# Attention bounds in wider passes, a new table of tiles, and earlier fillers in a fused attention and MLP kernel

## The chip, the cores and the metric

The kernel runs on one core of a Trainium2 chip. The core has five engines that run side by side and meet through semaphores: TensorE (PE, matmuls, whose weight loads the profile shows as PEld), VectorE (DVE), ScalarE (ACT), GpSimd (POOL) and SyncE (SP, which here only issues DMAs). The metric is the time of the whole program on the device in microseconds. The kernel before took 806.86 us, the median of 14 runs, which lie between 805.44 and 808.62.

## The reference

One layer norm feeds an attention block and an MLP; both results are added to the input. Attention has 32 heads of size 16 that share one set of keys and values. There are 2048 rows of width 512, and the MLP is 1792 wide.

```python
def _A_ref(x, wq, wk, wv, wo):
    q = (x @ wq).reshape(B, S, H, Dh).transpose(0, 2, 1, 3)
    k = x @ wk
    v = x @ wv
    scores = jnp.einsum("bhqd,bkd->bhqk", q, k) * (Dh ** -0.5)
    p = _softmax(scores, axis=-1)
    o = jnp.einsum("bhqk,bkd->bhqd", p, v)
    return o.transpose(0, 2, 1, 3).reshape(B, S, H * Dh) @ wo

def _B_ref(x, w1, b1, w2, b2):
    h = _gelu(jnp.einsum("bsd,df->bsf", x, w1) + b1)
    return jnp.einsum("bsf,fd->bsd", h, w2) + b2

xn = _layernorm(x, axis=-1)
return x + _A_ref(xn, ...) + _B_ref(xn, ...)
```

## The kernel before

**Tiles and units.** The rows of queries are cut into four token blocks of 512 (`NTB`, `TBW`), the heads into eight groups of four (`NGR`, `HG`), the keys into 16 tiles of 128 (`NT`). A score tile is one head, 128 keys and 512 queries: 128 x 512 numbers, which fill one bank of PSUM. There are 4 x 8 x 64 = 2048 of them, in the order token block, head group, key tile, head. Three successive tiles make a unit, so there are 683 units, some 171 for each token block and 21 for each head group. The scores of a unit are three matmuls (line 848), which go side by side into banks 0 to 2 or 3 to 5, by turns: the scores of unit u+2 can start once both engines have read the banks of unit u.

**Two ways to an exponential.** Most tiles go to ScalarE: one instruction (line 867) takes all such tiles of a unit, three or two, to the buffer `E`. In some units one tile, the first or the last, goes to VectorE instead[...]. It turns the scores into an integer whose bits, read as bf16, are a crude power of two (line 884, into `Dt`), and for batches of up to three tiles (`KB`) makes four shifted copies of it (line 899). Multiplied with five scaled copies of the values and summed, the five curves approximate the exponential. TensorE therefore has one matmul with values for a tile on ScalarE and five for a tile on VectorE, all at line 888, added up in bank 6. Which unit gives which tile to VectorE is written out in `DTAB`, a string with one character for each unit: a dot for none, 0 or 2 for the tile's place.

**Bounds.** Instead of a maximum over keys, softmax subtracts a bound that Cauchy and Schwarz give: it grows with the length of the query times the greatest length of a key. The queries of a head group are projected (`q_group`: 16 matmuls of line 563 into bank 7), copied to `QT` (line 742) and squared (line 744); the squares lie in slots 6 and 7 of the buffer `hb`, chosen by `sq`. `q_m` then sums the squares of a pair of groups with one small matmul each (line 557, into bank 7), takes a square root by integer arithmetic (line 970, into `mT`) and writes the result with four DMAs into a spare row of `QT`, so that the score matmul subtracts it by itself.

**Side work.** Everything else hangs beside the units. The list `side` says behind which unit's exp a piece may start: projections and bounds (`q_pair`), the two MLP layers (`h_mm`, then `h_chain` with the tanh of line 997, then `y_mm`), the output projection and stores (`out_tile`, `y_tile`). All these matmuls go to bank 7 too, which is one buffer, so each piece must be read out by VectorE before the next can start.

**What sets the order.** The kernel records all operations with what they read and write. `Prog.schedule` then gives every engine a fixed order, from costs and due times that are written in the code; `Prog.emit` puts a semaphore wait where an operand comes from another engine. Where its model of TensorE has a gap longer than `FILL_GAP`, and its own clock is past `FILL_FROM` microseconds, it puts in matmuls that add zeros (the filler, line 1169 in the profile), whose purpose is to keep the engine busy. Before the first values are projected, a second kind of filler runs (line 1167).

**The end of a group.** After 64 tiles `o_evac` copies bank 6 out (line 912), and the sums of the weights make a way through DRAM to become the rows of `rbc` (two halves by turns), by which line 923 divides. The very last group goes through `o_norm_last` instead: the reciprocals are spread over a buffer `rX` (line 949 on VectorE, line 951 on ScalarE) and transposed by TensorE.

Of the kernel before, what the change touches and what calls it, by code (L numbers as in the profile page):

```python
# [6 lines left out]
ACT = mybir.ActivationFunctionType  # L7
# [3 lines left out]
P = 128  # L11
# [17 lines left out]
D_FIRST = 3  # L29
FILL_GAP = 0.25  # L30
FILL_U = 0.8
FILL_FROM = 60.0
PV_MIN = 2
PV_S = 1
P1_ALLOW = -20.0
# [12 lines left out]
LCO = 0.0  # L48
PRO_FROM = 2.0
TBL = 1  # L50
DTAB = "....2..020..02..22...22.202220..20.00.0...220...222200..02200...2.02.2200.00220.02...20222.20...022.0000...2002.0.2.20000.000...2020.2220.0..20020....02.222.0022020..2...202.202202.02.222.....02.222.2022.000.22...20220.00.0222.2022...2220.02..2.2.0022......022...20.202002.2......02.0.000222.00.0..22.0..222..200000......2200.02202.000.22....2220.02.220.22220...22.2020.202202.022....2022.20022.0000.0....20222.220020....220..22..0...0.0..20.00.....022.20..20222.002....20220.20...22022.....0.20202.0.222.220....2220222.00222.2.22...222.0022.00222.0.20...2.020000.222.222.......202.0200.0...02......0...022...22.200....002.202...02.02.20...2022.22..20.020222...22202200..220.2000...."
Y_ALLOW = 8.0
H_ALLOW = 5.0
YT_ALLOW = (3,3,3,3)
# [371 lines left out]
def bass_parallel_sum__grouped_kv_mqa__dense_activation_gelu__prompt_kernel(  # L426
# [22 lines left out]
    TBW = 512  # L449
    NTB = S // TBW  # L450
    HG = 4
    NGR = H // HG
    NE, ND, KB = NE_ND_KB
    NOT, NPR = 3, 5
    NV = 1 + len(SPL_K)
    KZ = SPL_K.index(0)
    GAM = 128.0 / LN2 * 0.25
    bf, f32 = dt.bfloat16, dt.float32
    i16, i32 = dt.int16, dt.int32

    with ExitStack() as es:
        def sb(shape, dtype, name):
            return es.enter_context(nc.sbuf_tensor(name, shape, dtype))
# [23 lines left out]
        ident_f = sb([P, P], f32, "ident_f")  # L487
        selL = sb([P, 4], f32, "selL")
        rT = sb([P, 4, 4], f32, "rT")
        rX = sb([P, 4, P], f32, "rX")  # L490
        isc = sb([P, 1], f32, "isc")
        ibi = sb([P, 1], f32, "ibi")
        sel8 = sb([P, 8, 32], bf, "sel8")
# [20 lines left out]
        Vf = sb([P, NT, Dh], f32, "Vf")  # L514
        V1 = sb([P, NV, NT, 32], bf, "V1")
        QT = sb([P, NGR, TBW], bf, "QT")
        hb = sb([P, 8, TBW], bf, "hb")
        sqq = hb
        mT = sb([32, TBW], bf, "mT")
        E = sb([P, NE, TBW], bf, "E")  # L520
# [1 line left out]
        Of = sb([P, 2, TBW], f32, "Of")  # L522
        den = sb([P, 2, 16], f32, "den")
        rbc = sb([P, 2, TBW], f32, "rbc")
        rd_dram = nc.dram_tensor("rden_rows", [NTB * NGR, HG * TBW], f32).ap()
        oT = sb([P, NOT, TBW], bf, "oT")
        oTp = sb([P, NPR, TBW], bf, "oTp")
# [17 lines left out]
        def dve(fn, r=(), w=(), n=TBW, mode=1, allow=1.0, **kw):  # L545
            return add("dve", fn, r, w, occ=vcost(n, mode), lat=0.16, allow=allow, **kw)

        def act(fn, r=(), w=(), n=TBW, allow=0.0, **kw):
            return add("act", fn, r, w, occ=0.051 + n / 1.2e3, lat=0.22, allow=allow, **kw)
# [23 lines left out]
        for i in range(8):  # L573
            dma("sp", x_sb[:, 2 * i:2 * i + 2, :], x_view[:, 2 * i:2 * i + 2, :], f"d_x{i}",
                w=[("x", 2 * i), ("x", 2 * i + 1)], lat=2.3 + 0.5 * i, due=0.0)
# [8 lines left out]
        def setup(fn, r=(), w=(), occ=0.25, due=0.0, **kw):  # L584
# [18 lines left out]
              r=["wk_s", "wkp"], w=["wkp"], occ=0.45, due=2.0)  # L603
# [6 lines left out]
              r=["mrow"], w=["isc"], due=10.0)  # L610
        setup(lambda e: e.memset(crow[0:1, :], 1.13 * GAM * GAM), w=["crow"], due=10.0)
        setup(lambda e: e.memset(V1[:, :, :, Dh:32], 0.0), w=["V1"], occ=1.4, due=11.0)
        for v, c in enumerate((1.0,) + SPL_C):
# [3 lines left out]
              r=["mask4", "sel8"], w=["sel8"], due=12.0)  # L617
# [118 lines left out]
                          r=["wqp" if hq else "wqp0"] + tr(4 * tb, 4 * tb + 4), w=[B(bk)], **kw)  # L736

        def sq(hq):
            return 6 + hq % 2

        def q_evac(tb, hq, bk, **kw):
            dve(lambda e: e.tensor_copy(QT[:, hq, :], bank(bk)),  # L742
# [30 lines left out]
        for _, _, kind, a in sorted(steps, key=lambda s: s[:2]):  # L773
# [14 lines left out]
            r=[("std", LN_B[-1][0])] + ([("KT", ti) for ti in range(NT)] if TBL else []), w=["dum"], n=1600, due=1.0)  # L788
        dve(lambda e: e.tensor_reduce(kmx[:], kmax[:], AX.X, ALU.max), r=[("kmax", 0), ("kmax", NVA)], w=["kmx"], n=40, due=0.0)
        add("pe", lambda e: e.transpose(bank(3)[0:1, 0:P], kmx[:], ident_f[:]), r=["kmx", "ident_f"], w=[B(3)], occ=0.12, lat=0.22,  # L790
            due=0.0)
# [3 lines left out]
            r=["mrow"], w=[B(3), "ibi"], n=40, due=0.0)  # L795
        q_first_m(0, 7)
        dve(lambda e: e.tensor_copy(R2[:], bank(3)[:, 256:257]), w=[B(3), "R2"], n=40)
        for va, vb_ in ((0, NVA), (NVA, NT)):
# [3 lines left out]
                due=22.0)  # L802
            dve(lambda e, va=va, vb_=vb_: e.tensor_copy(V1[:, 0, va:vb_, 0:Dh], Vf[:, va:vb_, :]), r=["V1", ("Vf", va)], w=[("V", 0, va)],
                n=(vb_ - va) * Dh, due=22.1)
        for v, c in enumerate(SPL_C):
            setup(lambda e, v=v, c=c: e.tensor_scalar(V1[:, 1 + v, :, 0:Dh], Vf[:], c, None, ALU.mult),  # L806
                  r=["V1", ("Vf", 0), ("Vf", NVA)], w=[("V", 1 + v, 0), ("V", 1 + v, NVA)], occ=0.45, due=20.0)

        setup(lambda e: e.tensor_copy(wqp[:, :, 4:H, 0:Dh], wq_s[:, :, 64:D].rearrange("p k (h n) -> p k h n", n=Dh)),  # L809
              r=[("u", i) for i in range(8, 12)] + ["wqp"], w=["wqp"], occ=2.7, due=19.0, after=[pr.writer["ibi"]])  # L810
        setup(lambda e: e.tensor_scalar(sel8R[:], sel8[:], R2[:, 0:1], None, ALU.mult),
              r=["sel8", "R2"], w=["sel8R"], occ=0.5, due=22.0)
# [118 lines left out]
                    r=[("oT", gg % NOT)], w=[("oTp", pp % NPR, h, j)])  # L931

        def o_norm_last(gg):
            tb, g = divmod(gg, NGR)
            for h in range(2):
                c = slice(h * 256, h * 256 + 256)
                dve(lambda e, c=c: e.tensor_copy(Of[:, 0, c], pO[:, c]), w=["O", ("Of", 2 * h)], n=256, due=0.0)
            for h in range(2):
                for i in (2 * h, 2 * h + 1):
                    mm(bank(h)[:, 4 * i:4 * i + 4], Of[:, 0, i * P:(i + 1) * P], selL[:], True, True,  # L940
                       r=[("Of", 2 * h), "selL"], w=[B(h)], occ=0.2, due=0.0)
            for h in range(2):
                dve(lambda e, h=h: e.reciprocal(rT[:, 2 * h:2 * h + 2, :],
                                                bank(h)[:, 8 * h:8 * h + 8].rearrange("p (i j) -> p i j", j=4)),
                    w=[B(h), ("rT", h)], n=100, due=0.0)
                o = rX[:, 2 * h:2 * h + 2, :].rearrange("p i (j r) -> p i j r", j=4)
                i_ = rT[:, 2 * h:2 * h + 2, :].unsqueeze(3).to_broadcast([P, 2, 4, 32])
                if h == 0:
                    dve(lambda e, o=o, i_=i_: e.tensor_copy(o, i_), r=[("rT", h)], w=[("rX", h)], n=256, due=0.0)
                else:  # L950
                    act(lambda e, o=o, i_=i_: e.activation(o, i_, ACT.Copy), r=[("rT", h)], w=[("rX", h)], n=256, due=0.0)
            for h in range(2):
                for i in (2 * h, 2 * h + 1):
                    add("pe", lambda e, i=i, h=h: e.transpose(bank(h)[:, 128 + (i % 2) * P:256 + (i % 2) * P], rX[:, i, :], ident_f[:]),
                        r=[("rX", h), "ident_f"], w=[B(h)], occ=0.15, lat=0.22, due=0.0)
            for h in range(2):
                c = slice(h * 256, h * 256 + 256)
                dve(lambda e, h=h, c=c: e.tensor_tensor(oT[:, gg % NOT, c], Of[:, 0, c], bank(h)[:, 128:384], ALU.mult),
                    r=[("Of", 2 * h)], w=[B(h), ("oT", gg % NOT) if h == 0 else ("oTl", 1)], n=256, due=0.0)
# [6 lines left out]
        def q_m(tb, hqs, **rel):  # L966
            pq = tb % 2
            for n, hq in enumerate(hqs):
                mm(pM[0:32, :], sel8R[:, hq, :], sqq[:, sq(hq), :], n == 0, n == len(hqs) - 1, r=["sel8R", ("h", sq(hq))], w=[M4[0]], tp=(0, 0), kind="side", tag=(None, 0))
            dve(lambda e: e.tensor_scalar(mT[:].bitcast(i16), pM[0:32, :].bitcast(i32),  # L970
                                          0.5 / 65536.0, float(0x1fc00000) / 65536.0, ALU.mult, ALU.add),
                w=M4 + ["mT"], allow=EV_ALLOW)
            h0, n = hqs[0], len(hqs)
            for j in range(4):
                dst = QT[32 * j + 16:32 * j + 17, h0:h0 + n, :]
                dma("sp", dst, mT[8 * j + h0:8 * j + h0 + n, :], f"d_m{j}",
                    r=["mT"] + [("QT", hq) for hq in hqs], w=[("QTm", hq, j) for hq in hqs])
# [72 lines left out]
        def at(u, fn, cost=0.0):  # L1050
            side.append((u, len(side), fn, cost))

        def q_pair(tb, hqs, u):
            for i, hq in enumerate(hqs):
                at(u + 1.5 * i, lambda tb=tb, hq=hq: q_group(tb, [hq], {}), 0.93)
            at(u + 1.5 * len(hqs), lambda tb=tb, hqs=hqs: q_m(tb, list(hqs)), 0.6)

        q_pair(0, (1,), 0)
        q_pair(0, (2, 3), 3)
# [3 lines left out]
        for tb in range(NTB):  # L1063
            u0 = tb * UPT
            if tb > 0:
                for i in range(4):
                    at(u0 + 3 + (YS if tb < NTB - 1 else 9) * i, lambda tb=tb, i=i: out_tile(tb - 1, i), 0.6)
                q_pair(tb, (6, 7), u0 + 50)
            a, b = (HA, HB) if tb < NTB - 1 else (LA, LB)
            if tb == 0:  # L1070
                a = 18
            nf = FT if tb < NTB - 1 else FT - FIN_F
            for f0 in range(0, nf, 3):
                fts = list(range(f0, min(nf, f0 + 3)))
                for ft in fts:
                    at(u0 + a + (b - a) * ft / FT, lambda tb=tb, ft=ft: h_mm(tb, ft), 0.6)
                at(u0 + a + (b - a) * fts[-1] / FT, lambda tb=tb, fts=fts: h_chain(tb, fts), len(fts) * 1.067 + 0.33)
            if tb + 1 < NTB:
                for k in range(3):
                    q_pair(tb + 1, (2 * k, 2 * k + 1), u0 + 46 + 42.7 * k)  # L1080
            else:
                for i in range(4):
                    at(u0 + LS + LY * i, lambda tb=tb, i=i: y_tile(tb, i), 0.6)
                fts = list(range(nf, FT))
                for ft in fts:
                    at(u0 + LP + ft - nf, lambda tb=tb, ft=ft: h_mm(tb, ft), 0.6)
                if fts:
                    at(u0 + LP + len(fts), lambda tb=tb, fts=fts: h_chain(tb, fts, LAL), (len(fts) * 1.067 + 0.33) * LCO)
# [34 lines left out]
        for u in range(NU):  # L1123
# [4 lines left out]
            for t in ts:  # L1128
                gg, kt, j = tile_of(t)
# [78 lines left out]
```

## Time and profile before

| | us |
|---|---|
| median of 14 runs | 806.86 |
| the profiled execution | 805.68 |
| its span, from the first to the last instruction | 804.0 |
| ScalarE busy | 784.1 |
| TensorE busy | 772.1 |
| VectorE busy | 740.4 |
| weight loads | 241.9 |
| GpSimd busy | 21.8 |

The profile is of one execution. Lines name the engine, the source line, and output and input tiles; "mean ns" of a group is from the start to the end of one instruction, and successive instructions of ScalarE or VectorE overlap by a part of it. The first exp starts at 28.67 us, behind the layer norm, the projections of keys and values and the first queries; the last exp starts at 794.05 us, and what follows is the last normalisation, its projection and the last stores. The mean clock that TensorE was granted is 0.989 of full speed. The DMA engines matter for the first twenty microseconds, in which the inputs arrive; after that they move 5 to 32 GB/s.

### The profile page before, as it was taken

To read this page: it belongs to the slowest core of one execution; us is meant where nothing else is said; L and a number is where in the kernel's file an instruction comes from. 1 tells how busy PE (TensorE), PEld (TensorE's weight loads), DVE (VectorE), ACT (ScalarE), POOL (GpSimd) and SP (SyncE) were. 2 spreads that over 40 slices of the span, in tenths; PEclk is the share of its full clock that TensorE was granted. 3 is DMA by queue.
4 is the path that set the end of the run, shared out by engine and by line. 5 is a ranking of instruction groups with operands and counts; after the bars stand their busy time and mean duration, and the time that the engine had idled before them with its cause. 6 is when DMAs were issued, how large, how long until landed. Compare 5 with 4: busy or idle time off the path is not lost.

```text
span 804.0 us, 20982 instructions
## 1 busy us (share of the span) xinstructions
PE 772.1 (96%) x8946; PEld 241.9 (30%) x8946; DVE 740.4 (92%) x1409; ACT 784.1 (98%) x734; POOL 21.8 (3%) x81
## 2 busy tenths in 40 slices
PE   6799999999999999999999999999999999999997
PEld 4222322222333222332223322322332332332223
DVE  7499999999998999999999989999999987999896
ACT  5899999999999999999999999999999999999996
POOL 6400000000000000000000000000000000000000
PEclk8799999999999999999999999999999999999999
DMA  9000000000000000000000000000000001000001
GB/s 318 28 5 18 16 18 9 24 12 18 19 19 29 25 13 20 17 18 17 20 18 13 25 25 25 16 6 18 19 18 17 24 25 32 6 18 16 19 5 44
DMA packets 28023, 21.17 MB, mean 26 GB/s; under 512 B 14369, under 2 KB 23450, under 8 KB 27930
## 3 DMA queue, kind: packets, MB, share of 16 engines
q1 hardware_dynamic: 26346, 19.27, 8.2%
q8 instruction: 71, 1.16, 0.6%
q10 hardware_dynamic: 1584, 0.56, 0.3%
q14 instruction: 22, 0.18, 0.1%
HBM read 15.05 MB, written 2.35 MB: 22 GB/s over the span
## 4 chain that ended last, share of the span: by engine, by line
ACT 89%; PE 8%; DMA 1%; POOL 1%; DVE 0%; issue 0%; ACTq 0%; DVEq 0%
ACT E L867 84%; ACT ub L997 3%; PE pAll L888 3%; PE pAll L848 2%; PE pAll L563 2%; DMA ub<-in_A_wq_dram 1%; PE pAll L557 1%; ACT ub L687 1%; ACT xnT L705 0%; POOL V L806 0%; POOL wqp L809 0%; ACT KT L719 0%; PE pAll L700 0%; DVE x_sb L1159 0%; ACTq L570 0%
## 5 line engine op out<-in xcount | busy, mean ns | idle before, releaser
L867 ACT ACTIVATE E<-pAll 128x1024 bf16<-128x1024 f32 (+1 forms) x683 | 746.6, 1359 | 1.1 <-PE pAll L848 1.0
L888 PE MATMUL pAll<-Dt,V 128*32 128x512 bf16 x2080 | 362.6, 383 | 0.3
L884 DVE TENSOR_SCALAR Dt<-pAll 128x512 int16<-128x512 f32 x416 | 281.2, 687 | 27.8 <-PE pAll L848 26.4
L888 PE MATMUL pAll<-E,V 128*32 128x512 bf16 x1632 | 300.0, 388 | 0.4 <-DVE Of L912 0.4
L899 DVE TENSOR_SCALAR Dt<-Dt 128x1536 int16<-128x1536 int16 (+2 forms) x588 | 285.9, 533 | 0.7
L848 PE MATMUL pAll<-QT,KT 32*128 32x512 bf16 x2048 | 268.6, 386 | 17.1 <-ACT E L867 9.4
L848 PEld LDWEIGHTS pAll<-QT,KT 32*128 32x128 bf16 x2048 | 68.1, 91 | 295.6 <-ACT E L867 246.8
L888 PEld LDWEIGHTS pAll<-Dt,V 128*32 128x32 bf16 x2080 | 98.9, 94 | 97.8 <-issue 46.2
L563 PE MATMUL pAll<-w_sb,ub 128*32 128x512 bf16 x896 | 118.1, 382 | 0.2 <-DVE hb L983 0.2
L563 PE MATMUL pAll<-xnT,w_sb 128*32 128x512 bf16 x896 | 113.3, 382 | 0.3
L888 PEld LDWEIGHTS pAll<-E,V 128*32 128x32 bf16 x1632 | 71.2, 94 | 80.2 <-issue 66.2
L563 PE MATMUL pAll<-wop,oTp 128*32 128x512 bf16 x256 | 54.3, 381 | 0.0
L983 DVE TENSOR_SCALAR hb<-pAll,b1T 128x512 bf16<-128x512 f32 x56 | 41.9, 748 | 2.7 <-PE pAll L563 1.8
L563 PE MATMUL pAll<-xnT,wqp 128*32 128x512 bf16 x496 | 41.3, 394 | 0.8 <-POOL wqp L809 0.6
L563 PEld LDWEIGHTS pAll<-xnT,w_sb 128*32 128x32 bf16 x896 | 31.2, 95 | 20.4 <-issue 5.7
L563 PEld LDWEIGHTS pAll<-w_sb,ub 128*32 128x32 bf16 x896 | 32.4, 95 | 13.8 <-issue 5.4
L1169 PE MATMUL pAll<-xnT,zeros 128*32 128x512 bf16 x332 | 35.5, 383 | 0.0
L997 ACT ACTIVATE ub<-ub 128x1536 bf16<-128x1536 bf16 (+1 forms) x20 | 31.9, 1595 | 0.0
L742 DVE CAST QT<-pAll 128x512 bf16<-128x512 f32 x32 | 21.9, 686 | 7.0 <-PE pAll L563 6.7
L912 DVE COPY Of<-pAll 128x512 f32<-128x512 f32 x31 | 21.3, 687 | 5.4 <-PE pAll L563 4.5
L923 DVE TENSOR_TENSOR oT<-Of,rbc 128x512 bf16<-128x512 f32 x31 | 21.3, 687 | 0.0
L994 DVE TENSOR_TENSOR ub<-hb 128x1536 bf16<-128x1536 bf16 (+1 forms) x20 | 18.1, 905 | 0.2
(119 smaller groups left out, 280.4 us busy)
## 6 DMA issues: line engine op xcount, KB each, us to landing
rbc<-rden_rows SPq DMA_DIRECT2D x124, 64.0 KB, 2.0
w_sb<-in_B_w_dram SPq DMA_DIRECT2D x2, 1792.0 KB, 12.8
x_sb<-in_A_x_dram SPq DMA_DIRECT2D x8, 256.0 KB, 5.9
out_dram<-x_sb SPq DMA_DIRECT2D x16, 128.0 KB, 1.7
oTp<-oT SPq DMA_DIRECT2D x124, 16.0 KB, 1.8
QT<-mT SPq DMA_DIRECT2D x60, 2.0 KB
ub<-in_A_wq_dram ACTq DMA_DIRECT2D x1, 512.0 KB, 6.3
wop<-in_A_wo_dram SPq DMA_DIRECT2D x1, 512.0 KB, 15.7
```

What stands on the lines that cost most here:

```text
L563: add("pe", lambda e, c=c, j=j: e.matmul(o[c, :], l[:, c], rh, start=start, stop=stop, tile_position=(0, 32 * j)), r, [(k, j) for k in w] ...
L742: dve(lambda e: e.tensor_copy(QT[:, hq, :], bank(bk)), w=[B(bk)] + [(B(bk), j) for j in range(4)] + [("QT", hq)] + [("QTm", hq, j) for j i ...
L848: ins = e.matmul(o, l, rh, start=True, stop=True, tile_position=(q0, 0))
L867: exps.append(act(lambda e: e.activation(E[:, s0:s0 + na, :], bank(b0, na).rearrange("p (a n) -> p a n", a=na), ACT.Exp, scale=LN2 / 128.0 ...
L884: dve(lambda e: e.tensor_scalar(Dt[:, KZ, s, :], bank(bk), float(127 * 128) + SPL_D, SPL_MIN, ALU.add, ALU.max), w=[B(bk), ("D", s, KZ)], ...
L888: add("pe", lambda e, a, b: e.matmul(pO[32 * j:32 * j + 32, :], V1[:, v, kt, :], rhs, start=a, stop=b, tile_position=(0, 32 * j)), r=r + [ ...
L899: dve(lambda e, k=k: e.tensor_scalar(Dt[:, k, s0:s0 + n, :], Dt[:, KZ, s0:s0 + n, :], float(SPL_K[k]), None, ALU.add), r=[("D", s0 + i, KZ ...
L912: dve(lambda e: e.tensor_copy(Of[:, i, :], pO), w=["O", ("Of", i)], allow=0.0)
L923: onorm[gg] = dve(lambda e: e.tensor_tensor(oT[:, gg % NOT, :], Of[:, i, :], rbc[:, i, :], ALU.mult), r=[("Of", i)] + [("rbc", i, j) for j ...
L983: dve(lambda e: e.tensor_scalar(hb[:, ft % 6, :], pM, b1T[:, ft:ft + 1], None, ALU.add), r=["b1T"], w=M4 + [("h", ft % 6)], allow=ev)
L997: act(lambda e: e.activation(uu, uu, ACT.Tanh, scale=GELU_K), r=uk, w=uk, n=c, allow=al - 0.5, kind="tanh")
L1169: pr.filler = lambda e, j, o: e.matmul((pO if o else pM)[32 * j:32 * j + 32, :], zeros[:, 0:32], xnT[:, 0, 0:TBW], start=not o, stop=not o ...
```

## The change

Five things change together.

- `q_m` may take four head groups in one pass. In `q_pair` a new argument `ms` says for which groups it is called, and for none if it is empty. For the token blocks after the first, the bounds of groups 0 to 3 are made together after the second pair of projections, those of groups 4 to 7 together after the last pair, whose place moves from unit 50 to unit 40 of its block. The first block keeps its four passes.
- The squares get a ring of four slots (`NSQ`), 6 to 9 of `hb`.
- `rX` loses its own buffer and lies on the second half of `rbc`; both writers name that half as written.
- `FILL_FROM` goes from 60 to 30.
- `DTAB` is a different string of the same length; 426 of its characters are digits, where the old one has 416.

```diff
-FILL_FROM = 60.0
+FILL_FROM = 30.0
...
-DTAB = "....2..020..02..22...22.202220..20.00.0...220...222200..02200...
+DTAB = "...00.0020..2.0202....00022022..2002.0.0...000...0.02.02.2220...
...
-    NOT, NPR = 3, 5
+    NOT, NPR, NSQ = 3, 5, 4
...
-        rX = sb([P, 4, P], f32, "rX")
...
-        hb = sb([P, 8, TBW], bf, "hb")
+        hb = sb([P, 6 + NSQ, TBW], bf, "hb")
...
+        rX = rbc[:, 1, :].rearrange("p (i r) -> p i r", i=4)
...
-            return 6 + hq % 2
+            return 6 + hq % NSQ
...
+            RB1 = [("rbc", 1, j) for j in range(HG)]
...
-                    dve(..., r=[("rT", h)], w=[("rX", h)], n=256, due=0.0)
+                    dve(..., r=[("rT", h)], w=[("rX", h)] + RB1, n=256, due=0.0)
                 else:
-                    act(..., r=[("rT", h)], w=[("rX", h)], n=256, due=0.0)
+                    act(..., r=[("rT", h)], w=[("rX", h)] + RB1, n=256, due=0.0)
...
-        def q_pair(tb, hqs, u):
+        def q_pair(tb, hqs, u, ms=None):
             for i, hq in enumerate(hqs):
                 at(u + 1.5 * i, lambda tb=tb, hq=hq: q_group(tb, [hq], {}), 0.93)
-            at(u + 1.5 * len(hqs), lambda tb=tb, hqs=hqs: q_m(tb, list(hqs)), 0.6)
+            ms = hqs if ms is None else ms
+            if ms:
+                at(u + 1.5 * len(hqs), lambda tb=tb, ms=ms: q_m(tb, list(ms)), 0.6)
...
-                q_pair(tb, (6, 7), u0 + 50)
+                q_pair(tb, (6, 7), u0 + 40, (4, 5, 6, 7))
...
-                    q_pair(tb + 1, (2 * k, 2 * k + 1), u0 + 46 + 42.7 * k)
+                    q_pair(tb + 1, (2 * k, 2 * k + 1), u0 + 46 + 42.7 * k, (0, 1, 2, 3) if k == 1 else ())
```

The table is shown to its 64th character. As the program orders the instructions, VectorE has 426 instructions of line 884 and 10 of line 970 after the change (416 and 16 before), and SyncE issues 40 DMAs from `mT` to `QT` (64 before).

More of the change, by code (lines that the diff above doesn't have):

```diff
@@ L50 @@
 TBL = 1
-DTAB = "....2..020..02..22...22.202220..20.00.0...220...222200..02200...2.02.2200.00220.02...20222.20...022.0000...2002.0.2.20000.000...2020.2220.0..20020....02.222.0022020..2...202.202202.02.222.....02.222.2022.000.22...20220.00.0222.2022...2220.02..2.2.0022......022...20.202002.2......02.0.000222.00.0..22.0..222..200000......2200.02202.000.22....2220.02.220.22220...22.2020.202202.022....2022.20022.0000.0....20222.220020....220..22..0...0.0..20.00.....022.20..20222.002....20220.20...22022.....0.20202.0.222.220....2220222.00222.2.22...222.0022.00222.0.20...2.020000.222.222.......202.0200.0...02......0...022...22.200....002.202...02.02.20...2022.22..20.020222...22202200..220.2000...."
+DTAB = "...00.0020..2.0202....00022022..2002.0.0...000...0.02.02.2220...2022.20222.220.202...200.00.00.20.000.20..20.02.0.22000.02000...202.22.002.0.00.20....220..00022002.2.20...0002.02022.0.2220....222222.22.22020.00...22222.22.00.2.000.0..220...2.0220..0202....22202.020.2.22.222...202..0...2.02200.2...22.0.2..2..00..2000...22.0022.00.2002.02...20220.02.2202.2020...2222.20.202202.2220...2022.200220..0.00....222.0..2022.20.0.20....200.02.20.0..0200....2.220..220.200.02....222.20...02000.200..2.000..0222222.020....2202.22002022..022...2222.02.020222.2.20..222200.0202.222.22.....2..20.2.202.2..0.......0...2202..220.20..2.0..20.0..2.200000...0200.2.2200.00202....22022200..020.2000...."
 Y_ALLOW = 8.0
@@ L933, in o_norm_last @@
         def o_norm_last(gg):
-            tb, g = divmod(gg, NGR)
+            RB1 = [("rbc", 1, j) for j in range(HG)]
             for h in range(2):
@@ L948, in o_norm_last @@
                 if h == 0:
-                    dve(lambda e, o=o, i_=i_: e.tensor_copy(o, i_), r=[("rT", h)], w=[("rX", h)], n=256, due=0.0)
+                    dve(lambda e, o=o, i_=i_: e.tensor_copy(o, i_), r=[("rT", h)], w=[("rX", h)] + RB1, n=256, due=0.0)
                 else:
-                    act(lambda e, o=o, i_=i_: e.activation(o, i_, ACT.Copy), r=[("rT", h)], w=[("rX", h)], n=256, due=0.0)
+                    act(lambda e, o=o, i_=i_: e.activation(o, i_, ACT.Copy), r=[("rT", h)], w=[("rX", h)] + RB1, n=256, due=0.0)
             for h in range(2):
```

## The prediction

> **What bounds the kernel now.** I read, in this order, the busy shares and slices, the chain that ended last, the groups by form, the waits, and the order of each engine by time around the start.
>
> ```profile
> PE 772.1 (96%) x8946; PEld 241.9 (30%) x8946; DVE 740.4 (92%) x1409; ACT 784.1 (98%) x734; POOL 21.8 (3%) x81
> PE   6799999999999999999999999999999999999997
> DVE  7499999999998999999999989999999987999896
> ACT  5899999999999999999999999999999999999996
> ACT 89%; PE 8%; DMA 1%; POOL 1%; DVE 0%; issue 0%; ACTq 0%; DVEq 0%
> L867 ACT ACTIVATE E<-pAll 128x1024 bf16<-128x1024 f32 x417 | 423.9, 1198 | 0.4 <-PE pAll L848 0.3
> L867 ACT ACTIVATE E<-pAll 128x1536 bf16<-128x1536 f32 x266 | 394.0, 1611 | 0.7 <-PE pAll L848 0.6
> L884 DVE TENSOR_SCALAR Dt<-pAll 128x512 int16<-128x512 f32 x416 | 281.2, 687 | 27.8 <-PE pAll L848 26.4
> L899 DVE TENSOR_SCALAR Dt<-Dt 128x1536 int16<-128x1536 int16 x512 | 262.1, 555 | 0.7
> L1169 PE MATMUL pAll<-xnT,zeros 128*32 128x512 bf16 x332 | 35.5, 383 | 0.0
> ```
>
> ScalarE (ACT) is the bound: 98% busy, 89% of the chain, and idle before its exps for only 1.1 us. VectorE (DVE) follows at 92%. TensorE's 96% is less than it seems: 332 of its matmuls are fillers that compute nothing. An end minus a start overstates an exp, since successive ones overlap; I therefore took the distance between starts of successive ACT instructions in the timeline. It is 1.331 us after a three-tile exp (128x1536), 0.904 us after a two-tile exp (128x1024), 1.374 and 0.946 us after the two forms of the tanh. Then 266 x 1.331 + 417 x 0.904 + 16 x 1.374 + 4 x 0.946 = 756.8 us of ACT work, with no stall. The first exp starts at 28.67 and the last at 794.05; the starts exceed that work by 9.5 us in all: 1.3 in the first 34 units, 8.2 spread evenly over the other 649 (0.3 to 0.9 in every 43 units or so). This is what a change can win or lose besides the work itself.
>
> At the start it is another engine. The chain and TensorE's timeline show it:
>
> ```profile
> 31.35 1.04 PE pAll L563 x8
> 32.40 0.54 PE pAll L848 x3
> 32.94 0.98 PE pAll L563 x8
> 33.91 0.54 PE pAll L848 x3
> 34.46 0.55 PE pAll L888 x4
> ...
> 39.64 20.93 ACT E L867 x19
> 30.00:40.00 10.00, 9.26 (x72) 1.78 (x72) 3.35 (x6) 9.35 (x9) 4.12 (x6) 0.56 0.02 6
> 40.00:50.00 10.00, 9.96 (x119) 2.77 (x115) 9.97 (x20) 10.00 (x10) 0.00 (x0) 1.00 0.03 7
> ```
>
> From 31.35 to 39.6 the chain is matmul after matmul, at a granted clock of 0.56 (last number but two of the window rows); from 39.64 it is exp after exp.
>
> **What the Trainium skill says.** "ScalarE: Activation LUTs", What ACT_TABLE_LOAD costs: an ACTIVATE with immediates takes 186 ns + 0.833 ns per element, of which about 93 overlap back to back; that is 946 and 1373 ns for 1024 and 1536 elements, the tanh's distances to a nanosecond; the exps from PSUM are some 42 ns shorter, and I use the measured ones. "TensorE: Matmul & The Clock Gate", Part 1: the array runs at half clock until about one 3.4 us window of activity; the trace has half clock from 29.4 to 39.6 us, three such windows, and full clock from there to the end. "Perfetto Trace Analysis", Identifying the Most-Contended Engine: matmul busy time is a bad measure of TensorE; the fillers agree. "VectorE: DVE Perf Modes", Why PSUM operands drop a tier: fp32 from PSUM runs at one element a cycle; the trace has 0.598 us between starts for 512 elements from PSUM (L884) against 0.465 us for 1536 int16 elements in SBUF (L899).
>
> **The change part by part.**
>
> *Tile table.* I counted it: 426 units give a tile to VectorE, 416 before. So 427 exps have two tiles and 256 have three (417 and 266): ten times 1.331 - 0.904 = 0.427, **-4.27 us of ACT**, on the path everywhere except where ACT was not the bound. VectorE gets ten L884 more (10 x 0.598 = 6.0). Batches of three go from 128 to 132, of two from 13 to 12, single ones stay at 6: 16 more L899 of 0.465, 4 fewer of 0.334, +6.1. TensorE gets 50 Dt matmuls for 10 E matmuls: 40 more, four side by side in about 0.22 us, 2.2 us beside its fillers. Nothing.
>
> *Bounds in one pass of four.* The bound evictions (L970) go from 16 to 10, six times 0.600 (distance between starts; 670 ns duration): -3.6 us of DVE. The 31 small matmuls stay; SP issues 40 QT<-mT DMAs for 64. The bounds are never awaited now (no wait names that DMA) and the passes come some 40 units before their first scores, so nothing shows on the end. A pass waits for four squares instead of two, and it holds bank 7 no longer, since squares are ready by then: cost nothing, at worst a bank 7 round trip of about a microsecond that side work absorbs.
>
> *Rings and aliases.* Four slots for squares cost space only. The buffer rX on top of rbc can delay the last normalisation: ACT's copy (0.41 us at 797.66) now also comes after DVE's copy of 0.29 us. DVE already does that copy before the reciprocal ACT waits for (797.20 and 797.42), so 0, at worst 0.2.
>
> *Fillers.* 332 before and after by the instruction order; the first stands now behind the scores of 29 units instead of 43. Both places are far past 39.6 us where the clock is full. So this part does next to nothing: 0, and it cannot touch the half-clock start.
>
> *Start.* The new table gives tiles to VectorE in units 3, 4, 6, 7 and 8; the old in 4, 7 and 8. That is 2 x 0.427 = 0.85 of the 4.27, in the stretch where TensorE is the bound. Before the scores of unit 9 TensorE now has 8 L563 matmuls more (32 for 24; the next group of queries comes wholly before them), two rounds of about 0.43 at half or 0.22 at full clock. Unit 9's scores left at 40.07 and its exp at 40.56; I take these 0.3 later for this, and the 0.85 is not gained: **+1.2 given back**, between 0.5 (the clock is full early enough) and 1.9.
>
> *Stalls in steady state.* By the same durations and the order of instructions, VectorE's work from its first L884 on is 703 us before and 712 after (6.0 + 6.1 - 3.6 = 8.5, and one query copy of 0.6 that now comes after the first L884); ACT's is 756.8 and 752.5. VectorE's share of ACT's work goes from 92.9 to 94.6%. In the 16 stretches of about 43 units the highest are 1.035, 0.989 and 0.972 before; after, 1.008, 1.005, 1.004, 1.004 and 0.985. The old 1.035 (units 128 to 170) had a stall of just 0.56 us: work that is not urgent waits. And nearly all stalls sit behind a two-tile exp, where its 0.904 us must hold the release, the scores and 0.44 from scores to exp; units of this kind that follow each other directly are 281 before, 278 after. So the stalls should stay about the same: **+0.4**, from -1.5 (the new places suit better) to +3 (VectorE is late in four tight stretches rather than one).
>
> Sum: -4.27 + 1.2 + 0.4 = **-2.7 us**. The profiled execution took 805.68 (span 804.0 and 1.68 around it), so 803.0; the median of the runs shown is 806.86, 1.18 above it, so 804.2 for the median.
>
> **Rivals.**
> 1. *The stalls shrink too*: the passes saved free bank 7 and VectorE, the start loses only 0.5. -4.27 + 0.5 - 1.2 = -5.0, 801.9. For: six round trips fewer. Against: of 53 stalls over 40 ns, 30 had scores waiting last for an exp, not for VectorE.
> 2. *Given back* (no change): start 1.9, stalls +2, -0.4, 806.5. For: ten more tiles load VectorE by 8.5 us net. Against: even stalls before, whatever the stretch's load.
> 3. *VectorE becomes the bound* (slower): it waited 26.1 us for scores after 39.6 us, 3.7% of its 703. If it has this dead time in the tight stretches too, their need is 1.0 x 1.037 of ACT's. Four stretches of about 47 us by 3.7% are 7 us, and with the start 7 + 1.2 - 4.27 = +3.9, 810.8. It decides from 5.9 us of new stall or start loss on. Against: the stretch of 1.035 shows none of it.
> 4. *It doesn't do what it says*: holds for the fillers as shown; for the other parts the order has the new counts.
>
> **How the numbers follow.** Chances: forecast 0.50, rival 1 0.16, rival 2 0.23, rival 3 0.11. What this kernel's measurement can tell from no change is about 0.2%, or 1.6 us: faster is below 805.25, slower above 808.47. Faster has the forecast and rival 1, with a little from the forecast's edge going to no change and as much back from rival 2: 0.66; no change 0.23; slower 0.11. The range: low -4.27 + 0.5 - 0.9 = -4.7, so 802.2, with some 0.05 below; high 807.4, between no change and slower, with 0.15 above, taking the stalls' +3 and the start's 1.9 together (+0.6).
>
> **What would show it.** In the changed profile: 427 and 256 exps at the same distances between starts; ACT's share of the chain still near 89% with the PE stretch at the start as long or longer (first exp of the unbroken row at 39.6 or later, unit 9 near 40.9); 10 L970; the L884 wait for scores shorter than 26 us; the clock full from about 40 us to the end. Wrong would be: ACT idle or late by well over 9 us after unit 34 with DVE named as the releaser (rival 3), a stretch at half clock in the middle, or a later first exp, for which I see no reason since nothing before 28.67 us moves.

## The result, and the profile after

The changed kernel took 803.17 us, the median of 10 runs from 802.42 to 804.19, against 807.52 us for the kernel before in the runs beside it (47 runs, 805.44 to 809.38). The ratio is 0.9946, with a 95% interval from 0.9936 to 0.9956: it is faster by 0.54%, or 4.35 us. The profiled execution took 803.02 us, of which 801.3 are its span.

The page of the changed kernel, with the busy times, the slices of the granted clock and the chain by engine, then the groups:

```profile
PE 773.9 (97%) x8986; PEld 242.0 (30%) x8986; DVE 747.7 (93%) x1425; ACT 779.9 (97%) x734; POOL 21.8 (3%) x81
...
PEclk8899999999999999999999999999999999999999
...
ACT 80%; PE 11%; DVE 6%; DMA 1%; POOL 1%; issue 0%; ACTq 0%; DVEq 0%
```

```profile
L867 ACT ACTIVATE E<-pAll 128x1024 bf16<-128x1024 f32 x427 | 432.5, 1174 | 0.9 <-PE pAll L848 0.9
L867 ACT ACTIVATE E<-pAll 128x1536 bf16<-128x1536 f32 x256 | 380.2, 1592 | 0.5 <-PE pAll L848 0.4
...
L884 DVE TENSOR_SCALAR Dt<-pAll 128x512 int16<-128x512 f32 x426 | 288.0, 688 | 29.2 <-PE pAll L848 28.4
...
L899 DVE TENSOR_SCALAR Dt<-Dt 128x1536 int16<-128x1536 int16 x528 | 270.4, 555 | 0.7
```

ScalarE (ACT) is busy 4.2 us less than before, VectorE (DVE) 7.3 us more, and ScalarE still ends most waits. The chain that ended last now has 6% of VectorE in it, where it had none: at a few places VectorE is the one that is late. The granted clock is full from 36.7 us until the end.

It helps to cut an execution into four parts: what comes before the first exp; ScalarE's own work between the starts of the first and the last exp, from the counts and the distances between starts; the rest of that stretch, here called stall; and the tail from the start of the last exp. All parts are taken from the starts in the trace. Two executions of each kernel are shown, the second pair from the experiments:

| us | before | before again | changed | changed again |
|---|---|---|---|---|
| start of the first exp | 28.67 | 28.70 | 29.78 | 29.95 |
| ScalarE's work | 755.88 | 755.88 | 751.61 | 751.61 |
| stall, units 0 to 33 | 1.31 | 0.69 | 1.41 | 1.40 |
| stall, later units | 8.19 | 8.19 | 8.70 | 8.60 |
| tail | 9.92 | 9.89 | 9.80 | 9.81 |
| span | 804.0 | 803.4 | 801.3 | 801.4 |

(The work stops at the start of the last exp, so it is 0.90 less than the 756.8 of the prediction.) The work falls by the 4.27 us that were counted: the trace has 427 and 256 exps, and the median distances between starts, 0.904 and 1.331 us, are those of before. The stalls after unit 33 give back 0.4 to 0.5 us. The first exp starts anywhere from 28.7 to 30.0 us in the executions of this study, whatever the kernel, and both executions of the kernel before lie at the early end.

### The profile page after: what moved, and what is told of

Same layout as the page of the kernel before. It is cut to its first block, busy times and chain, and to the rows that moved or that the text cites. A ratio compares the mean times of both kernels' runs of the same rounds, so it can differ in the third digit from the quotient of the medians.

```text
span 801.3 us, 21071 instructions
## 1 busy us (share of the span) xinstructions
PE 773.9 (97%) x8986; PEld 242.0 (30%) x8986; DVE 747.7 (93%) x1425; ACT 779.9 (97%) x734; POOL 21.8 (3%) x81
## 4 chain that ended last, share of the span: by engine, by line
ACT 80%; PE 11%; DVE 6%; DMA 1%; POOL 1%; issue 0%; ACTq 0%; DVEq 0%
ACT E L867 77%; PE pAll L888 4%; PE pAll L563 3%; PE pAll L848 3%; ACT ub L997 2%; DVE Dt L899 1%; DVE Dt L884 1%; DMA ub<-in_A_wq_dram 1%; DVE hb L983 1%; PE pAll L557 1%; ACT ub L687 1%; ACT xnT L705 0%; DVE ub L999 0%; POOL V L806 0%; DVE ub L994 0%
## 5 line engine op out<-in xcount | busy, mean ns | idle before, releaser
L888 PE MATMUL pAll<-Dt,V 128*32 128x512 bf16 x2130 | 370.5, 383 | 0.4
L884 DVE TENSOR_SCALAR Dt<-pAll 128x512 int16<-128x512 f32 x426 | 288.0, 688 | 29.2 <-PE pAll L848 28.4
L899 DVE TENSOR_SCALAR Dt<-Dt 128x1536 int16<-128x1536 int16 (+2 forms) x600 | 292.8, 535 | 0.7
L563 PE MATMUL pAll<-w_sb,ub 128*32 128x512 bf16 x896 | 122.3, 382 | 0.0
L563 PE MATMUL pAll<-xnT,w_sb 128*32 128x512 bf16 x896 | 111.0, 382 | 0.3
L563 PE MATMUL pAll<-wop,oTp 128*32 128x512 bf16 x256 | 48.7, 381 | 0.1
L563 PE MATMUL pAll<-xnT,wqp 128*32 128x512 bf16 x496 | 39.4, 390 | 0.6 <-POOL wqp L809 0.6
L1171 PE MATMUL pAll<-xnT,zeros 128*32 128x512 bf16 x332 | 36.7, 383 | 0.0
L912 DVE COPY Of<-pAll 128x512 f32<-128x512 f32 x31 | 21.2, 685 | 0.1
L999 DVE TENSOR_TENSOR ub<-ub,hb 128x1536 bf16<-128x1536 bf16 (+1 forms) x20 | 18.1, 907 | 0.1
```

The source lines that it names most:

```text
L563: add("pe", lambda e, c=c, j=j: e.matmul(o[c, :], l[:, c], rh, start=start, stop=stop, tile_position=(0, 32 * j)), r, [(k, j) for k in w] ...
L884: dve(lambda e: e.tensor_scalar(Dt[:, KZ, s, :], bank(bk), float(127 * 128) + SPL_D, SPL_MIN, ALU.add, ALU.max), w=[B(bk), ("D", s, KZ)], ...
L888: add("pe", lambda e, a, b: e.matmul(pO[32 * j:32 * j + 32, :], V1[:, v, kt, :], rhs, start=a, stop=b, tile_position=(0, 32 * j)), r=r + [ ...
L899: dve(lambda e, k=k: e.tensor_scalar(Dt[:, k, s0:s0 + n, :], Dt[:, KZ, s0:s0 + n, :], float(SPL_K[k]), None, ALU.add), r=[("D", s0 + i, KZ ...
L912: dve(lambda e: e.tensor_copy(Of[:, i, :], pO), w=["O", ("Of", i)], allow=0.0)
L1171: pr.filler = lambda e, j, o: e.matmul((pO if o else pM)[32 * j:32 * j + 32, :], zeros[:, 0:32], xnT[:, 0, 0:TBW], start=not o, stop=not o ...
```

## The experiments

Three theories were set against each other. *Counting*: the change is worth the exp work that the table takes from ScalarE, and the rest is small. *Passes*: the wide passes bring the gain, by freeing bank 7 and VectorE. *Fit*: the table belongs to one fixed order of all engines, and is worth its count only there.

**One part at a time.** (Here and below a table is shown to its 64th character.) The first kernel has the new table alone, the second everything but the new table and the fillers.

```diff
@@ kernel before @@
-DTAB = "....2..020..02..22...22.202220..20.00.0...220...222200..02200...
+DTAB = "...00.0020..2.0202....00022022..2002.0.0...000...0.02.02.2220...
```

> The kernel before with the new table alone (426 units with a tile on VectorE, 16 passes for the bounds, FILL_FROM 60). Counting theory: the table takes 10 x 0.427 = 4.27 us from ScalarE whatever else is there, VectorE bears 3.6 us more than in the full change, so ratio to the kernel before 0.995 to 0.9965, stalls after unit 34 within 2 us of the full change's. Passes theory: the passes bring the gain by freeing bank 7 and VectorE; the table alone stays above 0.998. Fit theory: a table fits only the schedule it was made with; stalls grow by 3 us or more, ratio 0.998 to 1.003.

```diff
@@ changed kernel @@
-DTAB = "...00.0020..2.0202....00022022..2002.0.0...000...0.02.02.2220...
+DTAB = "....2..020..02..22...22.202220..20.00.0...220...222200..02200...
-FILL_FROM = 30.0
+FILL_FROM = 60.0
```

> The changed kernel with the old table and FILL_FROM 60, so only the passes of four, the ring and the alias are new; ScalarE's work is that of before, 756.8 us. Counting theory: ratio 0.999 to 1.001, stalls within 1 us of before's 8.2 after unit 34. Passes theory: 0.995 to 0.998, stalls fall by 2 to 4 us. Fit theory: stalls grow by 2 to 5 us, 1.002 to 1.006.

Measured: the table alone 825.42 us, ratio 1.0222 (1.0208 to 1.0236); the passes alone 827.63 us, 1.0243 (1.0221 to 1.0266). Alone, the two parts lose 18 and 20 us where together they win 4. Only the fit theory had the direction in both, and it had asked for a quarter of the size or less. The counted work is as it should be in both (751.61 and 755.88); the loss is stall and tail. In the passes-alone kernel nearly all of it is stall, 29.8 us; 13.1 of these lie behind units 255, 425 and 426, of which more below. ScalarE at the first of them:

```profile
321.51 2.37 ACT L867 ACTIVATE E<-pAll 128x1536 bf16<-128x1536 f32 x2 [8.45 <-PE pAll L848]
```

In the table-alone kernel the stall is 21.5 us, 11.4 more than in the changed kernel, and the tail 21.2 us, 11.5 more. The stall is spread, the longest single one being 1.3 us, and was not followed further. Its chain in the last stretch shows where the tail comes from (start, duration, what):

```profile
811.02 0.70 DVE x_sb L1037
...
811.76 3.96 PE pAll L563 x68
...
815.75 0.70 DVE x_sb L1037
...
816.49 4.82 PE pAll L563 x84
```

The last exp starts at 802.90, and then matmuls of the second MLP layer and the output, which belong beside the exps, still go through bank 7 one eviction (L1037) at a time. The side work had fallen behind.

**Fillers and start.**

```diff
@@ changed kernel @@
-FILL_FROM = 30.0
+FILL_FROM = 60.0
```

> The changed kernel with FILL_FROM back at 60: four fillers fewer, at unit 29, and the rest in the same order. Counting theory: the same as the changed kernel within its interval, 0.9936 to 0.9956. Rival: earlier fillers set the clock at the start; then half clock lasts three windows (10.2 us) again and the time rises by about 1 us, 0.996.

Measured: 803.35 us, 0.995 (0.9937 to 0.9962). The four fillers are worth nothing that can be told.

```diff
@@ changed kernel @@
-DTAB = "...00.0020
+DTAB = "....2..020
```

(Only the first ten characters are shown; the others are the same.)

> The changed kernel with the first 10 characters of the old table: units 3 and 6 are whole on ScalarE again, 424 tiles on VectorE, ScalarE 0.85 us more work. If TensorE at half clock bounds the start, as the prediction has it, those two units bring nothing: ratio within 0.001 of the changed kernel (0.9946), and unit 9 comes no later after the first exp than the changed kernel's 11.2 us. If ScalarE bounds it there too, 0.85 us or 0.1% slower, 0.9957, unit 9 near 11.9 us.

Measured: 806.83 us, 0.9995 (0.9985 to 1.0004): 0.45% slower than the changed kernel, four times what the two tiles are worth to ScalarE. Neither answer was right. Unit 9 comes 12.02 us after the first exp instead of 11.21; but the half clock lasted 10.2 us here and 6.8 in the changed kernel, so this pair does not show what the two tiles earn at the start. And then single stalls of 1.35, 1.74 and 1.12 us stand behind units 29, 123 and 162, where the changed kernel has none that long. Behind all three the scores wait for L884. Ten characters at the start moved the order of VectorE a hundred units later.

**Ten small misfits.** Ten tiles go one unit later, at units 60, 124, 180 and so on; no count changes.

Characters 57 to 72 of the changed kernel's table, with the first of the ten:

```diff
-.2220...2022.202
+.222.0..2022.202
...
```

> The changed kernel with ten of its 426 tiles for VectorE given one unit later, one in every 60 units. Counts of all instructions on ScalarE and VectorE are those of the change. Counting theory: ratio as the change, 0.993 to 0.997. Fit theory (a table is made for one fixed order; the two mixed kernels lost 20 us): ten small misfits are enough, 1.005 to 1.03, in a few long stalls rather than many short ones.

Measured: 827.13 us, 1.0247 (1.0228 to 1.0267). This separates fit from counting: same counts of every instruction on ScalarE and VectorE, 22.7 us more stall. TensorE's list is not quite the same. The kernel puts fillers where its own model sees a gap, and there are 496 of line 1171 for 332, of which 52 stand behind unit 425. So its own reckoning already had that hole; whether the fillers cost anything there was not tested. The stall is in few places, as expected: 5.43 us behind unit 255, 8.5 and 0.7 behind 425 and 426, 2.46 behind 596, then 1.74 and 1.12 behind 123 and 162, and smaller ones. VectorE in the timeline of that kernel, just ahead of the stall behind unit 123:

```profile
163.38 0.68 DVE L884 TENSOR_SCALAR Dt<-pAll 128x512 int16<-128x512 f32 x1
163.98 2.42 DVE L899 TENSOR_SCALAR Dt<-Dt 128x1536 int16<-128x1536 int16 x5
166.33 1.28 DVE L884 TENSOR_SCALAR Dt<-pAll 128x512 int16<-128x512 f32 x2
```

Five shifted copies stand ahead of the L884 (its first ends at 167.0) that frees the bank for the next scores, which start at 167.4. The order of VectorE is fixed in the program, so L884 cannot go first.

**The long gaps.** Units 256, 426 and 597 are the first with tiles of head group 4 in the second, third and fourth token block, whose bounds come from the pass for groups 4 to 7. (The expectations call the second 427; the gap behind unit 425 is the one before it.) In the changed kernel the eviction of that pass, its DMAs and the first scores that need them are

```profile
305.84 0.67 DVE L970 TENSOR_SCALAR mT<-pAll 32x512 int16<-32x512 int32 x1
```

```profile
306.53 2.51 SPq L570 DMA_DIRECT2D QT<-mT  x4
```

```profile
311.15 0.39 PE L848 MATMUL pAll<-QT,KT 32*128 32x512 bf16 x3
```

The eviction is behind the start of unit 251, five units ahead of unit 256. The plan has it at unit 213. And most of the five units goes to the DMAs: by the semaphore times in the trace, the last row that unit 256 awaits has landed at 309.57. So 1.6 us are to spare, one or two units; at units 426 and 597 it is 2.7 and 1.4 us. With ten tiles shifted, the same pass is evicted in units 255, 425 and 595 instead of 251, 420 and 593, and in the passes-alone kernel in 255, 425 and 593: the long gaps stand just where it comes late.

```diff
@@ changed kernel @@
-                q_pair(tb, (6, 7), u0 + 40, (4, 5, 6, 7))
+                q_pair(tb, (6, 7), u0 + 50, (4, 5, 6, 7))
```

> The changed kernel with the last pair of projections of a block, and its pass for groups 4 to 7, back at unit 50. In the changed kernel's trace that pass is evicted at unit 251, its first scores are unit 256, so the spare time is some 5 units, not the 40 of the plan. If so, ten units later the scores of group 4 must wait: a gap of 5 to 15 us with ScalarE idle before units 256, 427 and 597, ratio 1.02 to 1.05. If the plan's 40 units were real, no such gap, 0.994 to 1.005.

Measured: 841.9 us, 1.0435 (1.0417 to 1.0453), with 9.7 and 9.2 us of stall before units 256 and 426, and before unit 597 15.1, in two parts of 7.7 and 7.4 with a tanh between them. ScalarE and SyncE in the timeline, and the chain, around the first of them:

```profile
320.94 1.94 ACT L867 ACTIVATE E<-pAll 128x1024 bf16<-128x1024 f32 x2 [9.55 <-PE pAll L848]
```

```profile
317.38 2.48 SPq L570 DMA_DIRECT2D QT<-mT  x4
```

```profile
314.86 0.70 DVE QT L742
...
315.60 1.05 PE pAll L557 x4
...
316.68 0.69 DVE mT L970
...
317.41 1.15 PE pAll L563 x16
```

ScalarE idles 9.55 us until a matmul of the scores is done. The DMAs with the bounds are issued from 317.38 on; the last row that this unit awaits has landed at 320.37, and the scores start at 320.50. Before the issue the chain runs through the projection's copy, the four sums of squares and their eviction. This is the price of a pass that is late.

In the kernel with ten shifted tiles the rows have landed at 317.53, and the scores start only at 319.06. The chain there has side work between the two:

```profile
315.84 0.70 DVE QT L742
...
316.59 1.15 PE pAll L563 x16
...
317.76 0.70 DVE QT L742
...
318.51 0.61 PE pAll L563 x8
319.12 0.35 PE pAll L848 x3
```

TensorE's fixed order puts two projections and eight matmuls of the MLP before these scores, and each round waits until VectorE has emptied bank 7. At the three places the scores start 1.2 to 1.5 us after their bounds have landed. So the late pass makes most of such a gap, and the order around it the rest.

```diff
@@ kernel with ten shifted tiles @@
-                q_pair(tb, (6, 7), u0 + 40, (4, 5, 6, 7))
+                q_pair(tb, (6, 7), u0 + 30, (4, 5, 6, 7))
```

> The ten shifted tiles again, with the last pair of projections and its pass at unit 30 instead of 40. In the shifted kernel three gaps before units 256, 427 and 597 hold 17 of its 22.7 us of new stall; there the scores of group 4 wait for the bounds. Deadline theory: with the pass ten units earlier these three gaps shrink to under 1 us each, and the ratio falls from 1.025 to 1.003 to 1.015, what remains being VectorE late at other places (units 123 and 162). Rival (the shifted order is slow in itself, the gaps only show it): the total stays within 5 us, 1.018 to 1.025.

Measured: 819.98 us, 1.0159 (1.0141 to 1.0177). Neither answer came true, and there is something of both. The three gaps fall from 17.1 to 8.9 us (1.95, 6.23 and 0.7, none), which is nearly the whole fall of the stall, from 32.8 to 24.2; but they do not vanish. The eviction came at unit 253 in the second block, and at 425 in the third, where it had been before: the side list hands the pieces out in the order of their planned places, each needs bank 7, and a place ten units earlier in the plan moved the pass by few units or none. That the backlog of side work decides when a pass is made fits this, and was not tested alone. Part of the gain was lost again to a tail of 13.1 us instead of 11.1.

**Once more, for the start.** The two kernels unchanged, one profile each.

> The kernel before, once more, for its start: whether half clock lasts three windows (10.2 us) again and unit 9 comes 11.9 us after the first exp, and how much the time of the first exp (28.67 us) varies. If the clock's length at the start is chance, it may be two windows here; if the order of the start sets it, three.

> The changed kernel once more. If the order of the start sets the clock: half clock for two windows (6.8 us) again, unit 9 at 11.2 us after the first exp; if chance, three windows are as likely, and unit 9 near 11.9.

They took 805.07 and 803.09 us, one run each; their parts are in the table above. The granted clock in the windows of four executions (PE, PEld, DVE, ACT busy, then the clock; the kernel before, again, the changed one, again):

```profile
30.00:40.00 10.00, 9.26 (x72) 1.78 (x72) 3.35 (x6) 9.35 (x9) 4.12 (x6) 0.56 0.02 6
```

```profile
30.00:40.00 10.00, 9.44 (x79) 1.94 (x82) 3.93 (x7) 9.86 (x10) 3.94 (x6) 0.61 0.03 6
```

```profile
30.00:40.00 10.00, 7.25 (x64) 1.64 (x68) 5.07 (x9) 9.33 (x9) 5.23 (x7) 0.67 0.01 4
```

```profile
30.00:40.00 10.00, 7.36 (x66) 1.57 (x68) 4.72 (x9) 9.33 (x9) 5.31 (x8) 0.66 0.01 3
```

The half clock lasts 10.2 us in both executions of the kernel before and 6.8 in both of the changed one. The other profiles go with this: 6.8 us in all seven with the wide passes and the new start (in one the clock fell back, see below), 10.2 in all four with the old start. But the kernel with the new table alone and its refit below have the new start and 10.2 us; in the former the half clock began 1.3 us before the first exp, in the changed kernel with it or 0.5 us after it. So the order at the start is not all, and what sets the length stays open.

At a like clock the new start gains little. In the table-alone kernel the half clock ends 9.0 us after the first exp and unit 9 comes at 11.00; in the second execution of the kernel before they are 9.1 and 11.27. That is 0.27 of the 0.85 us that ScalarE saves there.

**Fitting again.** Three tables were fitted by equally many steps: one or two characters change, and the step is kept if the order that the kernel's own `schedule` makes gets no longer by its own reckoning.

The changed kernel, 136 characters different, 425 tiles for VectorE:

```diff
-DTAB = "...00.0020..2.0202....00022022..2002.0.0...000...0.02.02.2220...
+DTAB = "...00.0020..2.0202....000220.22.2002.00....020...0.00.002222....
```

> The changed kernel with 136 characters of its table changed one or two at a time, each kept if the kernel's own scheduler found the order no longer; 425 tiles on VectorE. ScalarE's work is 0.43 us more than in the change. Fit theory: the stalls fall from 10.1 to 8 to 9 us, ratio 0.992 to 0.9945. Counting theory alone: 0.9951.

The kernel before with the new table, 164 characters different, 421 tiles:

```diff
-DTAB = "...00.0020..2.0202....00022022..2002.0.0...000...0.02.02.2220...
+DTAB = "...00.0020..2.0002....00220002..2002.0.0...202...0.002..0022.2..
```

> The kernel with 16 passes and the new table (1.0222), its table refitted to that schedule by as many steps; 421 tiles on VectorE, so ScalarE's work is 5 x 0.427 = 2.1 us under before's. Fit theory: most of the 18 us comes back, ratio 0.998 to 1.008. Capacity theory (without the wide passes VectorE and bank 7 have no room for the tiles): it stays at 1.015 or more, with side work left after the last exp as in the unfitted run (21 us from the last exp to the end).

The kernel before, 128 characters different, 418 tiles:

```diff
-DTAB = "....2..020..02..22...22.202220..20.00.0...220...222200..02200...
+DTAB = "....2..22.0.20..02...22.202022..20.20.0...220...202020..0020..2.
```

> The kernel before with its own table refitted by as many steps; 418 tiles on VectorE, 0.85 us less for ScalarE. Fit theory: 0.9965 to 0.9985, part of the change's gain without the wide passes. If the passes are what makes room, the changed kernel refitted stays at least 0.3% faster than this one; if fitting is all, the two come within 0.2%.

Measured: the changed kernel refitted 804.37 us, 0.9962 (0.995 to 0.9974); the table with 16 passes refitted 808.47 us, 1.0017 (1.0008 to 1.0026); the kernel before refitted 806.03 us, 0.9981 (0.9972 to 0.9989). The second is the strongest evidence: 17 of the 18 us that the new table lost without the wide passes come back through the table alone. It also has five tiles fewer for VectorE; a table with as few that is not fitted was not run, so their share is open. Yet this kernel does not get under the kernel before, though ScalarE has 2.1 us less to do; its stall stays at 12.8 us, against 10.1 in the changed kernel. What the wide passes give is in this difference, and no run takes it apart. The third says that some of the gain, 0.2%, could be had without any other change. It was also to tell whether the passes make room (the changed kernel refitted at least 0.3% faster) or fitting is all (within 0.2%); the two are 0.21% apart, which decides nothing. The first is a miss: the refit does not beat the change. Its profiled execution was the slowest of its ten, 805.95 us. It has 9.4 us of stall after unit 33, no better than the changed kernel, and 2.8 us in the first 34 units, where the changed kernel has 1.4:

```profile
42.53 3.71 ACT L867 ACTIVATE E<-pAll 128x1024 bf16<-128x1024 f32 x3 [1.76 <-PE pAll L848]
```

```profile
40.00:43.00 3.00, 3.00 (x34) 0.73 (x26) 1.91 (x4) 1.24 (x2) 0.00 (x0) 0.58 0.04 7
```

There the clock fell back to half between 39.1 and 42.5 us. None of the kernels tried beats the changed one.

## Why the prediction was right, point by point

The forecast was -2.7 us, and a faster kernel was called likeliest; the measured 803.17 us (-4.35, interval -3.6 to -5.2) is inside the range, between the forecast and rival 1.

- *Tile table, -4.27 us of ScalarE*: shown, 755.88 to 751.61 by the counts and distances in the traces.
- *Stalls in steady state, +0.4 us*: the number held, 8.19 to 8.70 and 8.60, but by luck. It was worked out from the loads of long stretches, and ten tiles moved by one unit hardly change those, yet cost 22.7 us of stall. The range went up to +3.
- *Start, +1.2 us given back*: mis-sized. The stall of the first 34 units is 0.1 to 0.7 us above before's, by which pair is compared, and unit 9 comes 11.21 us after the first exp where before's two executions have 11.89 and 11.27. The eight more projection matmuls before unit 9's scores are not in the traces: 32 start before these scores in both kernels, so the 0.3 us for them had no ground. The step also kept the half clock as long as it had been, and it ended after 6.8 us; but that is not needed, as the table-alone kernel has 10.2 us of it and 1.20 us of stall there. That most of the 0.85 us is lost at the start holds at a like clock. Also, the half clock of before lay from 28.6 to 38.9 us, not from 29.4 to 39.6.
- *Rings, aliases and fillers, 0*: for the fillers shown by their removal; the tail is 9.8 us after 9.9, so the alias delays nothing that can be seen.
- *Bounds in one pass of four, nothing on the end*: the number held, the reason did not. "Some 40 units before their first scores" was read from the plan; the trace has five from the eviction, and 1.4 to 2.7 us from the landing of the DMAs. The trace of before could have told it: two passes planned for units 220 and 224 are evicted there in units 251 and 257. But groups 6 and 7 of that block, which the second of them serves, are not needed before unit 298; the wide pass also serves group 4, which is needed at 256. Ten units later it would have cost 39 us, as the place at unit 50 shows.
- *Rival 3, VectorE the bound*: not in the changed kernel, where L884 waits 23.1 us for scores after 39.6 us, hardly less than 26.1. But that share of work, on which it was argued, says little: the kernel with the passes alone has less VectorE work than before and lost 20 us.
- *Signs*: the L970 are 10, and the clock is full from 36.7 us. ScalarE's share of the chain was to stay near 89% and is 80%. A later first exp was named as a sign of being wrong, and it came, at 29.78 us; as it varies from 28.7 to 30.0 us over all kernels here, this tells nothing.
- What is left: the four parts put the difference at 3.0 to 3.8 us between the first and last exps, the medians at 4.35. The two executions of before whose profile is here took 805.68 and 805.07 us, under their median of 807.52, and began their first exp early. The granted clock of single runs may be a part of it. In the largest group of runs of the kernel before (47, median 807.53) the ten with a clock of 0.983 average 809.2 us and the six with 0.991 or more 805.9; of the changed kernel's ten runs nine have 0.991 or more, and these average 803.1. So 2.8 us separate the two at a like clock. In a smaller group of 17 runs of the kernel before the clock does not sort the times, and so this is not shown.

The prediction took the sum of the table for the change. That came out because the new table fits the order of the changed kernel, which the prediction allowed for only by -1.5 to +3 us of stall; the experiments show that a misfit costs four to six times the counted work. To that extent the right answer was luck.

## What to carry to other kernels

Where, as in this kernel, every engine has a fixed order and two are over 90% busy, count the work saved on the bounding engine first, then ask whether the order still fits: moving ten of 426 tiles by one unit cost 24 us where the whole change brought 4. Read the spare time of a step from the trace, as the distance from the landing of its last DMA to its first user, and not from its place in a plan: 43 units in the plan were 1.6 us. And do not judge the parts of such a change one by one without fitting each again: alone, each looked 2% slower, and the table, fitted again, 0.2%.

## What was not expected of the hardware

Half clock around the first exps lasted 6.8 or 10.2 us, and once 13.7 us, in the kernel before refitted; in the changed kernel refitted it lasted 6.8 and came back for 3.4. And well into some kernels single stretches of 3.4 to 6.8 us at half clock returned, as in the changed kernel refitted at 534 us:

```profile
530.00:540.00 10.00, 8.75 (x85) 2.25 (x83) 8.67 (x17) 9.14 (x9) 0.00 (x0) 0.83 0.01 2
```

ScalarE is idle for 0.86 us of those ten, and TensorE busy for 8.75. The kernel with the table alone had three such stretches, those with the passes alone and with the ten shifted tiles two each, the one with the pass at unit 50 none in spite of its long gaps. The kernel before and the changed one had none between the start and the last microseconds, in two profiles each.
